# A kernel of attention, eight experts and an MLP: two copies of an expert's products, 192 or 224 columns, chosen at run time by the length of its list

## The chip, the cores and the metric

The kernel is one program on one core of a Trainium2 chip. The metric is the device time of an execution in microseconds, median over several. The engines are PE (TensorE, the matrix engine; PEld is its loading of weights), DVE (VectorE), ACT (ScalarE), POOL (GpSimd) and SP (SyncE, here an issuer of DMAs). Each engine runs its own list of instructions in order and waits on semaphores for the others.

## The reference

Three stages follow one another, all in fp32 at the interface. The first is a decayed linear attention over 2 x 768 positions with 8 heads of 64. Its result, 1536 rows of 512, goes through a mixture of eight experts with one expert per row:

```
logits = xn @ en.T / tau                  # xn, en: rows scaled to length 1
expert_idx = np.argmax(logits, axis=1)
gate_w = probs[np.arange(N), expert_idx]
for e in range(E):
    mask = expert_idx == e
    h = np.maximum(x[mask] @ w1[e], 0.0)              # 512 -> 1024
    out[mask] = gate_w[mask, None] * (h @ w2[e])      # 1024 -> 512
```

The last stage is an MLP over all rows: `h = x @ w_in` (512 -> 2048), `g = elu(h)`, `g @ w_out`. The inputs come from a fixed seed. Worked out from them with the reference's own routing, the lists of the eight experts hold 188, 174, 195, 218, 200, 209, 177 and 175 rows.

## The kernel before, in words

**Products.** Every fp32 product is made of three f16 ones: each operand is split in a high and a low f16 part, and high x high, high x low and low x high are summed in PSUM. An expert's rows are gathered as columns of a tile with room for CAP = 224 of them; rows beyond 224 would be handled by an overflow loop at the end, which is empty for these inputs and is jumped over. Layer 1 of an expert (function `layer1`, line 949) is 96 matmuls of 128x128 weights against 224 columns: four groups `fp` of 24, each into one PSUM tile `ph`. Layer 2 (`layer2`, line 990) is 96 too, in two groups `mp2` of 48, each into one PSUM tile `py`. Each matmul has a weight load of its own. Behind each group ACT writes the high part of the result and DVE the low part, `h` (L957, L972) or `yT` (L996, L1000); the column at which an expert's part of `yT` begins is loaded by ACT and DVE from the table `offi` (L981).

**Order of the experts.** The loop over e emits layer 1 of expert e and then layer 2 of expert e - 1, so PE's order is L1(0), L1(1), L2(0), L1(2), L2(1) and so on to L1(7), L2(6), L2(7). Between groups, `tick` lets the generator `preparing` emit a bounded number of steps that split raw fp32 weights into f16 (ACT L157, DVE L161), and with them new loads of raw weights on SP (L135). The weights of the MLP are loaded and split in the same way.

**Routing.** In expert 0, after its second matmul group of 12, `route_end` makes the index lists (PE L758, DVE L762), and POOL gathers the rows of expert 1 (L769); for expert 1 PE transposes them (L933), for later ones a DMA does (L928). The generator `route_sorted` makes what else is needed of the lists. Its first step sums the routing masks (`ms`); the second adds them up over the partitions on PE (`op`, L784) and makes the counts `cnt` and the starts `off`, `offi` on DVE (L787 to L794). Its later steps sort the index list for the scatter of the output, write the gate values to memory and read them back as `bc` (DMAs of POOL), and make the overflow table (L1115 to L1152). Before the change layer 1 calls `next(self.sorting, None)` at the groups with odd `fp` of every expert from 1 on, and that is the only place where these steps are emitted.

**Tiles of PSUM.** `mm` takes a tile from a ring of four banks; the pool `ps_a` holds four more under the tag "acc", in turn for `py`, for small matmuls and, in the MLP, for the output's accumulators.

## Time and profile before

| | us |
|---|---|
| median of 3 runs (lowest, highest) | 506.09 (504.83, 507.26) |
| the profiled execution, its own time | 507.02 |
| its span in the trace | 505.1 |
| attention stage | 0 to 88.3 |
| expert stage | 88.3 to 245.9 |
| MLP stage, with the empty overflow loop | 245.9 to 505.1 |
| PE busy (share of the span) | 471.9 (93%) |
| DVE busy | 345.1 (68%) |
| ACT busy | 230.1 (46%) |

The profiled execution lies inside the range of the timed ones. Its mean granted clock of PE is 0.971 of full speed. The shares are means over three stages that differ; the rows further below are from single stages.

### The profile page before, as it was taken

The page shows a single profiled execution, that of the slowest core. Times are in us where ns is not written, and L with a number is a line of the kernel's source. Part 1 is how long each engine was busy: PE and PEld are TensorE (multiplying, and loading weights), DVE is VectorE, ACT ScalarE, POOL GpSimd, SP SyncE. Part 2 cuts the span into 40 slices and gives each one's busy share as a digit, 9 for nine tenths or more (in the row PEclk, how much of TensorE's full clock was granted, in tenths as well). Part 3 has the DMA queues.
Part 4 walks back from the last instruction along what each step waited for, and adds up shares of the span by engine and source line. Part 5 has one row for each costly group of instructions (what it writes and reads, how often), then busy time and mean ns, then how long its engine had stood idle before and what let it go on. Part 6 is the DMA issues. An engine that isn't in the chain of part 4 may idle for free. (4 is left out here: it accounts for less than half of the span.)

```text
span 505.1 us, 9103 instructions
## 1 busy us (share of the span) xinstructions
PE 471.9 (93%) x3678; PEld 332.3 (66%) x3678; DVE 345.1 (68%) x612; ACT 230.1 (46%) x382; POOL 73.0 (14%) x66
## 2 busy tenths in 40 slices
PE   6789976689999999999999999999999999999993
PEld 6688865589999999999644444444444444445561
DVE  3469775849999957999787897889544435345352
ACT  1156433768785665333364444535242333333341
POOL 4359520502103100000000000000000003003020
PEclk9799987979999999999999999999999999999997
DMA  6999923599999979956522220000000002002010
GB/s 220 377 404 405 404 96 126 202 283 307 303 381 295 345 289 307 328 182 215 190 84 83 84 84 1 0 1 1 0 1 0 1 0 84 0 2 84 1 62 27
DMA packets 27959, 79.09 MB, mean 157 GB/s; under 512 B 13280, under 2 KB 14848, under 8 KB 21768
## 3 DMA queue, kind: packets, MB, share of 16 engines
q1 hardware_dynamic: 25280, 70.63, 41.2%
q0 software_dynamic: 2288, 7.61, 4.2%
q8 instruction: 31, 0.51, 0.4%
q10 hardware_dynamic: 344, 0.21, 0.2%
q14 instruction: 16, 0.13, 0.1%
HBM read 68.33 MB, written 7.36 MB: 150 GB/s over the span
## 5 line engine op out<-in xcount | busy, mean ns | idle before, releaser
L1034 PE MATMUL pf<-yT,w 128*128 128x512 f16 (+2 forms) x672 | 133.4, 349 | 0.6 <-DVE yT L1000 0.6
L1074 PE MATMUL po<-w,g 128*128 128x512 f16 x576 | 133.3, 379 | 0.3 <-DVE g L1060 0.3
L1034 PEld LDWEIGHTS <-w 128*128 128x128 f16 x672 | 62.4, 98 | 66.0 <-issue 0.9
L1044 DVE TENSOR_TENSOR et<-pf,bc 128x512 f32<-128x512 f32 (+2 forms) x56 | 34.4, 615 | 97.0 <-PE pf L1034 94.8
L1074 PEld LDWEIGHTS <-g 128*128 128x128 f16 x576 | 55.9, 98 | 66.1 <-DVE g L1060 1.2
L1045 ACT ACTIVATE eu<-et 128x512 f32<-128x512 f32 (+2 forms) x56 | 31.9, 569 | 139.8 <-DVE et L1044 139.8
L161 DVE SCALAR_TENSOR_TENSOR w<-raw,w 128x1024 f16<-128x1024 f32 x64 | 76.6, 1228 | 17.8 <-ACT w L157 17.8
L949 PE MATMUL ph<-x,w 128*128 128x224 f16 x768 | 76.9, 262 | 0.5 <-DVE x L749 0.5
L949 PEld LDWEIGHTS <-w 128*128 128x128 f16 x768 | 74.6, 99 | 1.5 <-issue 0.7
L990 PE MATMUL py<-h,w 128*128 128x224 f16 x768 | 74.7, 259 | 0.0
L990 PEld LDWEIGHTS <-w 128*128 128x128 f16 x768 | 73.4, 98 | 0.2 <-issue 0.2
L157 ACT ACTIVATE w<-raw 128x1024 f16<-128x1024 f32 x64 | 64.4, 1051 | 2.2 <-DVE cs L882 2.1
L1093 POOL DMA_INDIRECT out<-o,idx x12 | 12.0, 1004 | 285.4 <-DVE o L1091 276.8
L769 POOL DMA_INDIRECT g<-rows,idx x16 | 22.8, 1428 | 91.0 <-DMA x<-g 60.0
L1060 DVE SCALAR_TENSOR_TENSOR g<-et,g 128x512 f16<-128x512 f32 (+2 forms) x56 | 34.0, 608 | 0.2 <-ACT g L1054 0.2
L1053 DVE SCALAR_TENSOR_TENSOR et<-eu,et 128x512 f32<-128x512 f32 (+2 forms) x56 | 33.9, 605 | 0.3 <-ACT eu L1046 0.3
L1046 ACT ACTIVATE eu<-eu 128x512 f32<-128x512 f32 (+2 forms) x56 | 31.9, 570 | 1.8
L1054 ACT ACTIVATE g<-et 128x512 f16<-128x512 f32 (+2 forms) x56 | 30.9, 552 | 0.2 <-DVE et L1053 0.2
L157 ACT ACTIVATE w<-cv 128x1024 f16<-128x1024 f32 x16 | 16.9, 1054 | 23.7 <-DVE cv L226 23.7
L957 ACT ACTIVATE h<-ph 128x448 f16<-128x448 f32 x32 | 16.7, 541 | 11.2 <-PE ph L949 11.2
L996 ACT ACTIVATE yT<-py 128x448 f32 (+1 forms) x16 | 8.7, 541 | 24.7 <-PE py L990 19.9
L226 DVE SCALAR_TENSOR_TENSOR cv<-raw,cv 128x1024 int32<-128x1024 int32 x16 | 19.5, 1220 | 0.2
(187 smaller groups left out, 405.8 us busy)
## 6 DMA issues: line engine op xcount, KB each, us to landing
raw<-w SPq DMA_DIRECT2D x32, 1024.0 KB, 6.8
in<-qkv SPq DMA_DIRECT2D x16, 512.0 KB, 6.7
raw<-wi SPq DMA_DIRECT2D x8, 1024.0 KB, 5.0
raw<-wo SPq DMA_DIRECT2D x8, 1024.0 KB, 5.1
win<-qkv SPq DMA_DIRECT2D x8, 512.0 KB, 10.6
rows<-row SPq DMA_DIRECT2D x16, 256.0 KB, 7.4
bc<-cd POOLq DMA_DIRECT2D x1, 768.0 KB, 7.7
Dm<-Z SPq DMA_DIRECT2D x1, 512.0 KB, 4.2
```

Source lines behind the costliest of these rows:

```text
L157: nc.scalar.activation(out=o[0], in_=x, func=AF.Copy, scale=sc)
L161: nc.vector.scalar_tensor_tensor(out=o[1], in0=x, scalar=sc, in1=o[0], op0=ALU.mult, op1=ALU.subtract)
L949: nc.tensor.matmul(ps[:, j, :], w[:, wl, k, c : c + P], x[:, xl * KD + k, :], start=(n == 0), stop=(n == 11))
L990: nc.tensor.matmul(ps[:, j, :], w[:, wl, f % 4, c : c + P], h[:, hl, f, :], start=(n == 0), stop=(n == 23))
L1034: nc.tensor.matmul(ps[:, :n], w[:, wl, k, c : c + P], yT[yl][:, k, t0 : t0 + n], start=(i == 0), stop=(i == 11))
L1044: nc.vector.tensor_tensor(out=t[:, :n], in0=UT[m, f][:, :n], in1=self.bc[:, t0 : t0 + n], op=ALU.mult)
L1045: nc.scalar.activation(out=u[:, :n], in_=t[:, :n], func=AF.Relu, scale=-1.0)
L1046: nc.scalar.activation(out=u[:, :n], in_=u[:, :n], func=AF.Exp, scale=-1.0)
L1053: nc.vector.scalar_tensor_tensor(out=t, in0=u, scalar=-1.0, in1=t, op0=ALU.add, op1=ALU.max)
L1054: nc.scalar.activation(out=g[:, 0, :n], in_=t, func=AF.Copy, scale=S_G)
L1060: nc.vector.scalar_tensor_tensor(out=g[:, 1, :n], in0=t, scalar=S_G, in1=g[:, 0, :n], op0=ALU.mult, op1=ALU.subtract)
L1074: nc.tensor.matmul(acc[t], g[:, gl, t * P : t * P + P], w[:, wl, f % 4, :], start=(f == first and i == 0), stop=(f == last and i == 2),)
```

## The change

For experts 1 to 7 PE's products of a layer exist twice in its program, over 192 and over 224 columns. Before each layer PE loads one number (`width[e]`, 1 where the list is longer than 192) and branches to one of the copies. The other engines have no second copy: the groups' waits and releases stand in both copies, so each group of 24 or 48 matmuls still releases its writers by itself. Expert 0 runs 224 columns without a branch. Since both copies write the same tiles, these are allotted once: four tiles `ph` in the ring's four banks, two `py` under a tag of their own, with two left for "acc". The width flags are made in `route_sorted` right behind `offi`; its first two steps are now emitted in expert 0 behind `route_end`, and with the calls in layer 1 left as they were, all later steps come one expert earlier.

```diff
+WIDTHS = (192, CAP)
+    def widths(self, e):
+        if e == 0:
+            yield CAP
+            return
+        i = self.nc.tensor.value_load(self.width[0:1, e : e + 1], min_val=0, max_val=len(WIDTHS) - 1)
+        with self.tc.If(i == 0) as narrow:
+            yield WIDTHS[0]
+        with narrow.Else():
+            yield WIDTHS[-1]
...
+        nc.vector.tensor_scalar(out=self.width, in0=self.cnt, scalar1=float(WIDTHS[0]), scalar2=None, op0=ALU.is_gt)
...
-        ps_a = pool("ps_a", 4, space=PSUM)
+        ps_a = pool("ps_a", 2, space=PSUM)
...
+        ph = [mm([P, 2, CAP], f"ph{i}") for i in range(4)]
+        py = [ps_a.tile([P, 2, CAP], F32, name=f"py{i}", tag="py") for i in range(2)]
...
-                ps = mm([P, 2, CAP], f"ph{e}_{fp}")
-                for j in range(2):
...
+                if fp == 0 or e == 0:
+                    hs = range(4) if e else [fp]
+                    pss = {i: ph[i] for i in hs}
+                    ws = {i: self.need(4 * e + i // 2) for i in hs}
+                    for cols in self.widths(e):
+                        for i in hs:
+                            for j in range(2):
...
+                                        nc.tensor.matmul(
+                                            pss[i][:, j, 0:cols], ws[i][:, wl, k, c : c + P], x[:, xl * KD + k, 0:cols],
...
+                    if e == 0 and fp == 0:
                         self.route_end(ps_a)
+                        next(self.sorting)
+                        next(self.sorting)
                         self.tick(3.0)
...
-            for mp2 in range(2):
-                ps = ps_a.tile([P, 2, CAP], F32, name=f"py{e}_{mp2}", tag="acc")
...
+            pss = py
+            ws = [self.need(4 * e + 2 + i) for i in range(2)]
+            for cols in self.widths(e):
+                for m in range(4):
```

On PE, layer 1 of expert 1 followed directly on the last group of expert 0 (`ph_3`, weights `w_523`):

```order
L949 LDWEIGHTS w_523
L949 MATMUL ph_3_1243<-x_946,w_523 128x224
L949 LDWEIGHTS w_896
L949 MATMUL ph_0_1279<-x_1215,w_896 128x224
L949 LDWEIGHTS w_896
L949 MATMUL ph_0_1279<-x_1215,w_896 128x224
```

At the same place of the changed program (its line 971 is the layer 1, 782 and 783 are the load and the branch):

```order
L971 LDWEIGHTS w_523
L971 MATMUL ph_1093<-x_946,w_523 128x224
L782 TENSOR_LOAD width
L782 ISA x2
L783 COMPARE_AND_BRANCH
L971 LDWEIGHTS w_896
L971 MATMUL ph_1090<-x_1241,w_896 128x192
L971 LDWEIGHTS w_896
```

Four instructions now stand between the two groups, and the first copy has 192 columns. On PE again, after 192 rows of the narrow copy of expert 1's layer 2 (line 1015) comes the jump over the wide copy:

```order
L1015 MATMUL py_1095<-h_1303,w_1563 128x192
L1015 LDWEIGHTS w_1563
L1015 MATMUL py_1095<-h_1303,w_1563 128x192
L783 UNCONDITIONAL_BRANCH
L1015 LDWEIGHTS w_1541
L1015 MATMUL py_1094<-h_1303,w_1541 128x224
```

That jump passes 192 rows of the wide copy and its closing branch, and lands on the head of layer 1 of expert 3, here with the wide copy's end before it:

```order
L1015 LDWEIGHTS w_1563
L1015 MATMUL py_1095<-h_1303,w_1563 128x224
L783 UNCONDITIONAL_BRANCH
L782 TENSOR_LOAD width
L782 ISA x2
L783 COMPARE_AND_BRANCH
L971 LDWEIGHTS w_1668
L971 MATMUL ph_1090<-x_1889,w_1668 128x192
```

PE's list as a whole goes from 6790 to 9548 rows. On DVE, behind the cast of the index list in expert 0, four splits of weights (L161) followed before:

```order
L762 CAST idx<-ip 128x16
L161 SCALAR_TENSOR_TENSOR w_896<-raw_427,w_896 128x1024
L161 SCALAR_TENSOR_TENSOR w_1138<-raw_492,w_1138 128x1024 x2
L161 SCALAR_TENSOR_TENSOR w_1145<-raw_526,w_1145 128x1024
L972 SCALAR_TENSOR_TENSOR h_1093<-ph_0_1094,h_1093 128x448
```

In the changed program the two steps of `route_sorted` and the width flags stand ahead of them:

```order
L764 CAST idx<-ip 128x16
L792 TENSOR_REDUCE ms<-M 128x8
L794 CAST ms_1145<-ms 128x8
L800 COPY cnt<-op 128x8
L801 MEMSET off 128x1
L803 TENSOR_TENSOR off<-off,cnt 128x1 x7
L805 COPY offf<-off 128x8
L807 CAST offi<-off 128x8
L809 TENSOR_SCALAR width<-cnt 128x8
L163 SCALAR_TENSOR_TENSOR w_896<-raw_427,w_896 128x1024
```

Fourteen instructions moved ahead of the splits (now L163), and `cnt` waits there for PE's small matmul `op`, which moved along.

## Rows read from the trace of the kernel before

**Rows 1.** Windows: span, us; busy us of each engine; PEclk; DMA share; GB/s.

```profile
88.30:245.90 157.60, 151.69 (x1579) 150.00 (x1579) 136.64 (x223) 94.10 (x125) 21.88 (x16) 0.98 0.88 284
201.70:248.20 46.50, 45.90 (x471) 44.91 (x469) 45.43 (x72) 16.62 (x24) 0.00 (x0) 1.00 0.72 233
245.90:505.10 259.20, 249.54 (x1250) 117.83 (x1248) 152.13 (x238) 102.88 (x185) 12.04 (x12) 0.99 0.10 33
```

**Rows 2.** Timeline of PE in the expert stage: start, us, then the group.

```profile
134.73 9.36 PE L990 MATMUL py<-h,w 128*128 128x224 f16 x96
143.93 9.36 PE L949 MATMUL ph<-x,w 128*128 128x224 f16 x96
...
227.52 18.56 PE L990 MATMUL py<-h,w 128*128 128x224 f16 x192
```

**Rows 3.** Timeline of PE near the end of the MLP.

```profile
484.44 0.83 PE L1034 MATMUL pf<-yT,w 128*128 128x128 f16 x12
485.11 2.11 PE L1074 MATMUL po<-w,g 128*128 128x512 f16 x9
```

**Rows 4.** Instructions of lines 1161, 981, 1182: ns min/median/max, first and last start.

```profile
L1161 PEldq TENSOR_LOAD <-nu x1: 487/487/487, 495.7 to 495.7; - x1
...
L981 DVEq FUSED_REGOPS  x7: 190/190/206, 138.9 to 239.4; - x7
...
L1182 PEldq COMPARE_BRANCH  x3: 101/197/3347, 496.4 to 501.9; - x3
```

**Rows 5.** The same view, line 949, from 159 to 162.3 us.

```profile
L949 PEldq EVENT_SEMAPHORE  x1: 51/51/51, 160.6 to 160.6; - x1
L949 PEld LDWEIGHTS <-w x1: 97/97/97, 162.2 to 162.2; 128*128 128x128 f16 x1
```

**Rows 6.** The same view, line 1182 (overflow loop), whole span, then 497 to 499.

```profile
L1182 DVEq COMPARE_BRANCH  x3: 41/51/61, 496.8 to 501.8; - x3
...
L1182 PEldq COMPARE_BRANCH  x1: 3347/3347/3347, 496.7 to 496.7; - x1
```

**Rows 7.** DMA queue of instructions: packets, MB, share; whole span, then 496.6 to 500.1.

```profile
q8 instruction: 31, 0.51, 0.4%
...
q8 instruction: 1, 0.02, 1.7%
```

**Rows 8.** Windows between starts of instruction packets (columns as in rows 1).

```profile
205.75:215.56 9.81, 9.81 (x105) 9.81 (x104) 9.05 (x33) 1.09 (x2) 0.00 (x0) 1.00 0.98 271
215.56:229.97 14.41, 14.41 (x153) 14.41 (x151) 14.31 (x18) 5.78 (x9) 0.00 (x0) 1.00 0.65 218
...
259.15:286.79 27.64, 27.64 (x130) 12.54 (x128) 22.24 (x29) 13.82 (x22) 0.00 (x0) 1.00 0.34 114
```

**Rows 9.** PE in the attention stage: timeline with idle time before, and windows.

```profile
65.42 0.18 PE L680 MATMUL kr<-oha,ohb 128*128 128x2 f16 x1 [2.11 <-DVE nrm L451]
...
65.80:69.20 3.40, 3.40 (x29) 3.16 (x26) 2.07 (x4) 0.55 (x1) 2.39 (x3) 0.50 0.24 58
...
81.09 0.17 PE L640 MATMUL kr<-M,c 128*128 128x8 f16 x1 [3.30 <-DVE M L629]
...
79.40:86.30 6.90, 5.21 (x47) 4.57 (x47) 3.35 (x13) 1.58 (x4) 0.00 (x0) 0.51 0.21 78
```

**Rows 10.** Timeline of DVE: list starts, overflow table (first and last), an eviction.

```profile
116.96 1.32 DVE L790 TENSOR_TENSOR off<-off,cnt 128x1 f32<-128x1 f32 x7
...
207.32 0.15 DVE L1115 TENSOR_SCALAR ov<-cnt 1x8 f32<-1x8 f32 x1
...
213.08 0.13 DVE L1152 CAST nu<-ce 1x1 int32<-1x1 f32 x1
...
237.56 0.61 DVE L1000 SCALAR_TENSOR_TENSOR yT<-py,yT 128x448 f32 x1
```

**Rows 11.** Timeline of PE in expert 0, with its waits for gathered rows.

```profile
98.32 0.62 PE L933 MATMUL pt<-c,g 128*128 128x128 f16 x8 [2.44 <-DMA g<-rows,idx]
102.33 0.82 PE L933 MATMUL pt<-c,g 96*128 96x96 f16 x8 [3.39 <-DMA g<-rows,idx]
```

## The prediction

> **What bounds the kernel now.** I read the stages first, in windows: in the expert stage TensorE (PE) is busy 151.69 of 157.60 us and in the MLP stage 249.54 of 259.20, at a granted clock of 0.98 and 0.99 [rows 1]. So in both stages the time is PE's instruction stream. VectorE (DVE) comes next: 136.64 of 157.60 us, and 45.43 of 46.50 in the last three experts [rows 1]. The timeline of PE then shows that stream as an unbroken row of 96-matmul groups, one group per layer and expert, the next starting 9.20 us after the last (134.73 to 143.93): 95.8 ns a matmul of 224 columns [rows 2]. Nothing that only relieves DVE, ACT or the queues can show; shorter matmuls can, and so can anything that makes PE's sequencer late.

> **Columns.** At the end of the program twelve matmuls of 128 columns, each with a weight load of its own, take from 484.44 to 485.11: 0.67/12 = 55.8 ns [rows 3]. Against 95.8 ns that is 40.0 ns for 96 columns, 0.417 ns a column, with no fixed part that would keep 192 columns from paying: 95.8 - 32 x 0.417 = 82.5 ns, 13.3 ns less. By the reference's own routing the eight lists hold 188, 174, 195, 218, 200, 209, 177 and 175 tokens; expert 0 always runs 224, so experts 1, 6 and 7 are narrow and 2 to 5 wide. 3 x 192 matmuls x 13.3 ns = **-7.7 us** (bounds -7 and -8). The most the change can give by its idea is thus 1.5%.

> **Heads.** Each of the 14 blocks (experts 1 to 7, two layers) begins on PE with a load of one number, two register instructions and a compare with branch. Nearest rows: PE's one load of a number took 487 ns, a pair of register instructions on DVE 190, PE's median branch 197 [rows 4]; about 0.9 us, 1.1 with gaps. PE's sequencer runs ahead of its array: a wait that it passed at 160.6 stands before a weight load that began at 162.2, 1.6 us later [rows 5]. While the head runs, the array works that queue off. I cost the heads at **0**, with the cover just wide enough; without it they would be 14 x 1.1 = +15 us.

> **Code.** This is the term that decides. PE's program grows from 6790 to 9548 rows, and a block takes 390 places in it (4 of head, 192 + 1, 192 + 1) of which it walks 197 and jumps 193. What does a jump cost? DVE's branches of the tail, the taken one over its part of the overflow loop among them, took 41 to 61 ns; PE's, over some 890 instructions of that loop, took 3347 ns [rows 6], and one packet of the instruction queue falls into it [rows 7]. The page's queue row has 31 such packets for 0.51 MB [rows 7], 16 KB each. Cut at the starts of these packets, the MLP stage has exactly 128 weight loads a piece, thus 256 instructions, one packet per 256; in the expert stage it has 104 to 151 [rows 8]. I read from this that code comes in pages of 256 instructions, that the next page is asked for when a page is entered, and that a page not there costs F, 3.35 us from the request on, of which PE has up to 1.6 us of lead to set against it. The uneven 104 to 151 say that the request is served up to 24 pairs (2.3 us) late where the other queues are full (DMA share 0.98 in the stretch with 104, 0.34 in the quiet one) [rows 8]; so F lies between 3.35 and 5.65 there. Before, a page lasts 256 x 47.9 ns = 12.3 us and nothing of it shows. After, 390 places go by in 8 to 9 us, a page in 5 to 6, and a page that holds a skip whole is left after 63 places, 3.0 us.

> A narrow block jumps at its end, over the wide copy; a wide one at its start, over the narrow copy. Where a wide block follows a narrow one, the two jumps are five instructions apart and skip 386 places, a page and a half. By the order of the layers this happens twice: second layer of expert 1 to first layer of expert 3 (about 150 us), and first layer of 6 to second layer of 5 (about 217 us). The page landed on was asked for only on reaching those five instructions, so PE stands for F less what is left of its lead. I walked the whole list of PE's instructions with these rules, page by page. At F = 3.35 it waits 2.2 and 1.7 us at the two double jumps and 0.5 elsewhere: 4.4. At F = 4.7, it waits 3.6 and 3.0 there and five times 0.3 to 0.9 after single jumps, where 3.0 us of walking and a lead not yet rebuilt fall short: **+9.5**. At 5.65 some 17. I take 4.7, nearer to the full queues, since the share is still 0.98 up to 215 us and 0.65 after [rows 8].

> [...]

> **Clock.** A stall also has an aftermath. PE stood 2.11 us before 65.42, and the stretch from 65.80 to 69.20 then ran at 0.50, the lower of the two levels; it stood 3.30 us before 81.09, inside a stretch of 6.90 us at 0.51 [rows 9]. Half speed costs half of those stretches, 1.7 to 3.4 us. Two stalls of 3 us or more: 3.4 to 6.8, and 0 if they stay well under 2.11. I take **+4**.

> **The moved routing steps.** The sums of the lists and the width flags go to expert 0, ahead of DVE's weight splits; the seven additions alone took 1.32 us at 116.96 [rows 10], all of it about 2.5. PE's small matmul for them comes up to 1 us late, before two waits of 2.44 and 3.39 us for gathered rows that are there anyway [rows 11], so it is hidden. Splits and with them the raw weight loads move back by the same 2.5 us, which can let those gathers land earlier: 0 to -3, taken as **-1**. The other steps come an expert earlier; the overflow table, DVE 207.32 to 213.08 [rows 10], with them, out of the stretch where DVE has least room.

> **Fixed banks.** The accumulators of the second layer are now two tiles instead of four. Only experts 6 and 7 run second layers back to back: 227.52, 192 matmuls [rows 2], so the last one starts at 236.7, and DVE emptied a tile of expert 6 only from 237.56 [rows 10]. With the overflow table gone from there DVE is earlier, with 7.9 instead of 9.2 us it has less time: 0 to +3, taken as **+0.5**.

> **The sum.** -7.7 + 0 + 9.5 + 4 - 1 + 0.5 = +5.3 on the profiled execution's 507.0, which stands 0.9 above the median of 506.1: 511.4, say **511.5 us**. With F from 3.35 without clock (506.1 - 8.2 + 4.4 = 502.3) to 5.65 with 6.8 of clock (521.7), this case alone reaches from 502 to 522.

> **The rivals.** *Code never late.* If more than the next page lies ready, the decisive point being 386 places of skip, no jump waits: 506.1 - 7.7 - 1 + 0.5 = 498, faster. For it: no wait for code can be seen in 12.3 us per page, and the packets' landing is not the request. Against it: PE's jump of 890 cost 3347 ns with a packet inside, so the store ahead ends before 890, and behind that jump no second packet came at once. [...] Chance 0.33. *The effects cancel*, 503.6 to 508.6: F near 3.35 with one of the two stalls followed by a low clock (502.3 + 1.7 to 3.4), or code in time but DVE, busy 45.43 of 46.50 us [rows 1], holds the narrow experts 6 and 7 to the old pace, which loses 5.1 of the 7.7 us: 503. Chance 0.17. *The flags do nothing*: were all lists over 192, the columns would give 0, the skips would all be single, and the time 506 to 509; the routing counts speak against it, under 0.02. *Heads uncovered* would add up to 15 us, to 525; the lead of 1.6 us speaks against it, 0.05, inside the forecast's side.

> **How the numbers follow.** About 0.5% (2.5 us) is what a measurement here can tell from no change: faster is below 503.6, slower above 508.6. The forecast has 0.5, nearly all of it slower; code in time 0.33, all faster; cancelled 0.17, some of it below 503.6. Faster 0.35, same 0.15, slower 0.50. The range must hold both sides: from 497.5, a little under the rival's 498, to 520, which leaves out only the upper end of the code term with the whole price of the clock.

> **What would show it.** Right: matmuls of experts 1, 6 and 7 at 82 to 83 ns, others at 95.8; two PE gaps of 2 to 4 us at about 150 and 217 us right behind a jump, with an instruction packet landing just before they end and a clock of 0.5 behind; packets 5 to 6 us apart. Wrong if the MLP stage begins 6 to 9 us before 245.9 with no gap at the jumps, or if PE stands at every head by about a microsecond, or if waits for DVE in experts 6 and 7 take the gain.

## The result and the profile after

| | before | after |
|---|---|---|
| median (lowest, highest), us | 505.46 (504.48, 507.26) | 511.32 (508.83, 512.58) |
| profiled execution, its span, us | 507.02, 505.1 | 511.16, 509.4 |
| expert stage on PE, us | 88.27 to 245.92 | 86.57 to 251.46 |

The ratio is 1.0106 (95% interval 1.0056 to 1.0155): slower by about 1%. All ratios here go by the runs within 1.5% of the fastest of their kernel; one kernel below had three longer ones. The window of the expert stage, span first, then busy time by engine, PE's granted clock, DMA share and GB/s, answer to [rows 1]:

```profile
86.57:251.46 164.89, 148.19 (x1580) 143.71 (x1580) 138.81 (x225) 94.92 (x125) 19.31 (x16) 0.97 0.85 273
```

The stage is 7 us longer, though PE is busy 3.5 us less in it. So matmuls did get shorter, and PE now stands idle. Where it stands is read in the timeline of PE of the changed kernel (start, us, line, count, and in brackets the idle time before and what ended it by the semaphores); it answers to [rows 2, 11]:

```profile
91.15 0.17 PE L797 MATMUL op<-ms,c 128*128 128x8 f16 x1 [1.59 <-DVE ms L794]
91.17 6.42 PE L971 MATMUL ph<-x,w 128*128 128x224 f16 x48
97.43 0.95 PE L952 MATMUL pt<-c,g 128*128 128x128 f16 x16
...
120.12 9.36 PE L971 MATMUL ph<-x,w 128*128 128x224 f16 x96 [2.12 <-ACT yT L1024]
129.32 8.08 PE L1015 MATMUL py<-h,w 128*128 128x192 f16 x96
141.99 11.02 PE L971 MATMUL ph<-x,w 128*128 128x224 f16 x96 [4.59 <-DVE w L163]
152.85 0.51 PE L877 MATMUL sp<-rhs,wohb 128*128 128x60 bf16 x12
153.37 3.82 PE L1015 MATMUL py<-h,w 128*128 128x224 f16 x38
157.45 5.72 PE L1015 MATMUL py<-h,w 128*128 128x224 f16 x58 [0.27 <-issue]
163.87 9.36 PE L971 MATMUL ph<-x,w 128*128 128x224 f16 x96 [0.70 <-ACT yT L1024]
...
173.50 3.05 PE L1015 MATMUL py<-h,w 128*128 128x224 f16 x30
180.66 7.95 PE L1015 MATMUL py<-h,w 128*128 128x224 f16 x66 [4.10 <-issue]
...
197.64 2.46 PE L1015 MATMUL py<-h,w 128*128 128x224 f16 x24
200.91 7.07 PE L1015 MATMUL py<-h,w 128*128 128x224 f16 x72 [0.81 <-issue]
207.82 8.08 PE L971 MATMUL ph<-x,w 128*128 128x192 f16 x96
215.74 1.89 PE L1015 MATMUL py<-h,w 128*128 128x224 f16 x18
219.14 7.65 PE L1015 MATMUL py<-h,w 128*128 128x224 f16 x78 [1.50 <-issue]
...
235.61 16.01 PE L1015 MATMUL py<-h,w 128*128 128x192 f16 x192 [0.91 <-ACT h L983]
```

Three things are to be seen. The transposes of expert 1 no longer wait for gathered rows: the 2.44 and 3.39 us of [rows 11] are gone, and a wait of 1.59 us for the moved sums has come ahead of them. A narrow layer takes 7.92 us (207.82 to 215.74) instead of 9.20: 82.5 ns a matmul. And behind expert 0 stand eight gaps, 15.0 us together, where [rows 2] had none. Some fall between two layers, at a seam, and carry the name of DVE or ACT, some in the middle of a copy with nothing to wait for ("issue").

The four in mid-copy are worth a count. PE's list of instructions has two places for a matmul and its weight load. From the gap after 30 matmuls of layer 2 of expert 3 to that after 24 of expert 4 it is 66 x 2 + 1 to the end of the copy, 390 for the block between, 4 of head, 193 of the copy jumped over, and 24 x 2: 768 = 3 x 256. From 38 of expert 2 to 30 of expert 3, and from 24 of expert 4 to 18 of expert 5, it is 768 again (116 + 1 + 390 + 4 for a small product + 4 + 193 + 60, and 144 + 1 + 390 + 4 + 193 + 36). With a packet per 256 instructions [rows 8] that is three pages each time, so I read these gaps as standing at page ends.

For the gaps at the seams, the durations of single branches at line 783 (min/median/max in ns, start in us):

```profile
L783 PEldq COMPARE_BRANCH  x1: 3116/3116/3116, 116.8 to 116.8; - x1
L783 PEldq COMPARE_BRANCH  x1: 4930/4930/4930, 136.9 to 136.9; - x1
...
L783 PEldq COMPARE_BRANCH  x1: 1703/1703/1703, 162.0 to 162.0; - x1
L783 PEldq COMPARE_BRANCH  x1: 317/317/317, 172.9 to 172.9; - x1
...
L783 PEldq COMPARE_BRANCH  x1: 1639/1639/1639, 233.1 to 233.1; - x1
```

Of the 20 branches of this line the six that fall through took 0.07 to 0.09 us and ten jumps 0.22 to 0.41; those at the gaps of 2.12, 4.59, 0.70 and 0.91 took 1.6 to 4.9. The granted clock behind the two longest gaps, in windows from the gap to the end of the group (columns as above):

```profile
142.00:152.90 10.90, 10.90 (x98) 10.25 (x99) 7.25 (x9) 5.13 (x7) 0.86 (x1) 0.84 1.07 334
180.66:188.44 7.78, 7.78 (x66) 7.21 (x67) 1.76 (x2) 1.49 (x2) 2.58 (x3) 0.81 0.77 282
```

Layer 1 of expert 3 takes 10.86 us from 141.99 to 152.85 instead of 9.20, and 66 matmuls 7.78 instead of 6.32: 3.1 us for the clock (0.61 from 142.00 to 145.40 and 0.56 from 180.70 to 184.10, most of it at the lower of the two levels in the trace, 0.50 and 1.00). Behind the other gaps the pitch is as ever: 9.20 us for the group after 2.12, 6.91 for 72 matmuls after 0.81.

### The profile page after: what moved, and what is told of

Read it like the earlier page. It is cut to its first block, busy times and chain, and to the rows that moved or that the text cites. A ratio compares the mean times of both kernels' runs of the same rounds, so it can differ in the third digit from the quotient of the medians.

```text
span 509.4 us, 9182 instructions
## 1 busy us (share of the span) xinstructions
PE 469.5 (92%) x3678; PEld 327.2 (64%) x3678; DVE 346.3 (68%) x613; ACT 230.9 (45%) x382; POOL 70.4 (14%) x66
## 5 line engine op out<-in xcount | busy, mean ns | idle before, releaser
L1062 PEld LDWEIGHTS <-w 128*128 128x128 f16 x672 | 62.4, 98 | 65.4 <-issue 0.2
L163 DVE SCALAR_TENSOR_TENSOR w<-raw,w 128x1024 f16<-128x1024 f32 x64 | 76.9, 1228 | 18.5 <-ACT w L159 18.4
L971 PE MATMUL ph<-x,w 128*128 128x224 f16 (+1 forms) x768 | 74.7, 261 | 8.0 <-DVE w L163 4.6
L1015 PE MATMUL py<-h,w 128*128 128x224 f16 (+1 forms) x768 | 73.1, 257 | 7.6 <-issue 6.7
L971 PEld LDWEIGHTS <-w 128*128 128x128 f16 x768 | 71.6, 100 | 11.6 <-issue 7.0
L1015 PEld LDWEIGHTS <-w 128*128 128x128 f16 x768 | 70.1, 99 | 9.7 <-issue 7.8
L771 POOL DMA_INDIRECT g<-rows,idx x16 | 20.2, 1266 | 72.7 <-DMA x<-g 42.7
L998 DVE SCALAR_TENSOR_TENSOR h<-ph,h 128x448 f16<-128x448 f32 x32 | 19.6, 616 | 2.0 <-ACT h L983 1.9
```

The lines of the kernel that those rows point to most:

```text
L163: nc.vector.scalar_tensor_tensor(out=o[1], in0=x, scalar=sc, in1=o[0], op0=ALU.mult, op1=ALU.subtract)
L971: nc.tensor.matmul(pss[i][:, j, 0:cols], ws[i][:, wl, k, c : c + P], x[:, xl * KD + k, 0:cols], start=(n == 0), stop=(n == 11),)
L1015: nc.tensor.matmul(pss[m // 2][:, m % 2, 0:cols], ws[f // 4][:, wl, f % 4, m * P : m * P + P], h[:, hl, f, 0:cols], start=(n == 0), stop=( ...
L1062: nc.tensor.matmul(ps[:, :n], w[:, wl, k, c : c + P], yT[yl][:, k, t0 : t0 + n], start=(i == 0), stop=(i == 11))
```

## The experiments

Theory A: PE waits for its own code, after jumps and in mid-copy. Rivals: B, the seams' gaps are data waits, as their releasers say; C, the moved steps and fixed banks are neutral, and the gather waits vanished by chance; D, the heads cost. For the vanished gather waits: E, the raw weight loads start later; F, the fixed banks; G, the steps' earlier place.

### Columns without a branch

```diff
     def widths(self, e):
...
+        yield WIDTHS[0] if e in (1, 6, 7) else CAP
```

> One copy of each layer's products and no branch; 192 columns for experts 1, 6 and 7 and 224 for the others are fixed when the program is built, which holds for these inputs' lists alone. Fixed banks and moved routing steps stay. Theory A (code pages that come late after jumps, and the low clock behind the two long ones, cost the 15 us of waits and some 3 us of clock seen in the changed kernel's trace): all gaps at the seams vanish, 511.3 - 15 - 1.3 (ends of the pipeline at the gaps) - 3 = 492 us, 491 to 494. Rival B (the gaps before layer 1 of experts 2, 3 and 4, which the trace puts down to DVE and ACT, are waits for split weights and evictions that come late in the new order): they stay, 8 us with their clock, and the time is 499 to 501.

Measured: 493.57 us, ratio to before 0.9746 (0.9715 to 0.9776). PE's timeline of this kernel has the same narrow layers and no idle time behind the transposes but 0.49 us:

```profile
102.59 8.08 PE L963 MATMUL ph<-x,w 128*128 128x192 f16 x96 [0.49 <-ACT x L945]
110.51 9.36 PE L1007 MATMUL py<-h,w 128*128 128x224 f16 x96
119.71 9.36 PE L963 MATMUL ph<-x,w 128*128 128x224 f16 x96
128.91 8.08 PE L1007 MATMUL py<-h,w 128*128 128x192 f16 x96
136.83 9.36 PE L963 MATMUL ph<-x,w 128*128 128x224 f16 x96
```

All eight gaps are gone, though nothing was taken out but PE's loads of a width, its branches and the second copies; DVE's width flags stand as before. B falls: a releaser is the semaphore that came last before the engine went on, and at 141.99 it had come during a wait for something else: the branch of 136.9 lasted up to 141.8.

### One copy of 224 columns

```diff
     def widths(self, e):
...
+        yield CAP
```

> One copy over 224 columns for every expert, no branch, no load of a width; fixed banks and moved routing steps stay. All theories that put the columns at 7.7 us: static columns plus 7.7. Theory A: 500 us (499 to 502), so 5 to 6 us under the kernel before, all of it from the two waits for gathered rows in expert 0 (2.44 and 3.39 us with their low clock) that are gone in the changed kernel. Rival C (those waits vanished by chance, the moved steps and fixed banks are neutral): 505 to 506.5.

Measured: 500.38 us, 0.9882 (0.9851 to 0.9913). Without any narrow column the moved steps and fixed banks alone gain 5.8 us; C falls. Against the fixed columns it is 6.8 us slower by the medians, the pitch says 7.7; the runs of each spread over 1.6 to 1.7 us.

### Two copies of 224 columns: alternating, and always the first

```diff
         with self.tc.If(i == 0) as narrow:
-            yield WIDTHS[0]
+            yield CAP
```

> The changed kernel with 224 columns in both copies; the compare, the branches and all jumps are the same, narrow experts take the first copy and wide ones the second. Theory A: the same page walk, a little slower pages in the three experts: 13 us of waits and 2 to 4 us of clock over the single copy, 514 to 518. Rival D (the heads, a load and a compare of about 0.7 us each on PE's sequencer, are what costs, not where the jump lands): the single copy plus 14 x 0.7 to 1.1, 510 to 516, equal to the kernel in which every block takes its first copy.

For the second kernel also:

```diff
-        nc.vector.tensor_scalar(out=self.width, in0=self.cnt, scalar1=float(WIDTHS[0]), scalar2=None, op0=ALU.is_gt)
+        nc.vector.tensor_scalar(out=self.width, in0=self.cnt, scalar1=float(N), scalar2=None, op0=ALU.is_gt)
```

> As the alternating kernel (two copies of 224 columns, same heads), but the width flag is set only above 1536, so all 14 blocks take their first copy and jump at their end: no two jumps ever follow each other without 197 instructions between them. Theory A: the two double jumps and their clock are gone, single jumps remain, 7 to 9 us of waits over the single copy: 506 to 510, and 6 to 9 us under the alternating kernel. Rival D: equal to the alternating kernel within 1.5 us.

Measured: alternating 522.93 us, 1.0339 (1.0302 to 1.0377); always the first copy 0.9993 (0.9965 to 1.0022), with seven runs from 502.63 to 507.46 us (median 506.02) and three more from 511.08 to 513.27 (all ten: 506.74). Same copies, same heads, the same work on PE, and 16 to 17 us between them: only where the branch goes differs. D alone can't give that. In the alternating kernel the long gaps stand at the seam of the first double jump and one page end behind the second:

```profile
145.08 11.96 PE L971 MATMUL ph<-x,w 128*128 128x224 f16 x96 [4.70 <-DVE w L163]
...
217.79 1.89 PE L1015 MATMUL py<-h,w 128*128 128x224 f16 x18
223.85 10.12 PE L1015 MATMUL py<-h,w 128*128 128x224 f16 x78 [4.17 <-issue]
```

Both are followed by a low clock (0.77 from 145.08 to 156.88 and 0.74 from 223.85 to 233.81; 11.96 us against the usual 9.36, and 10.12 for 78 matmuls against 7.65 in the changed kernel). The alternating kernel is 22.5 us over the single copy where I expected 15 to 17, the other 5.6 (6.4 by all ten runs) where I expected 7 to 9. Single jumps are not free; the kernel that has only these stands in mid-copy too, after 25 matmuls and 768 places later after 7 (142 + 1 + 193 + 390 + 24 + 4 + 14):

```profile
129.23 2.56 PE L1015 MATMUL py<-h,w 128*128 128x224 f16 x25
134.15 6.98 PE L1015 MATMUL py<-h,w 128*128 128x224 f16 x71 [2.36 <-issue]
...
150.97 0.83 PE L1015 MATMUL py<-h,w 128*128 128x224 f16 x7
153.58 8.70 PE L1015 MATMUL py<-h,w 128*128 128x224 f16 x89 [1.78 <-issue]
```

### Heads with short copies

```diff
-                    for cols in self.widths(e):
-                        for i in hs:
+                    for cols, i in ((c, q) for q in hs for c in (self.widths(e) if q == 0 else [CAP])):
```

(both copies of 224 columns; layer 2 likewise, by its four m)

> The same 14 heads (load, two register instructions, compare) as in the changed kernel, with the same alternation, but only the first 24 of a block's 96 matmuls stand in two copies, both of 224 columns; the other 72 stand once. Code grows by a quarter of what it grows in the change. Theory A: pages last 9 us or more, no waits: the 500.4 us of the single copy, 499.5 to 502. Rival D: 14 heads of 0.7 to 1.1 us exposed: 510 to 516.

Measured: 500.43 us, 0.9888 (0.9856 to 0.9921), against 500.38 without any head. Fourteen heads cost nothing that can be seen, as a lead like that of [rows 5] would have it. D falls for the change as it stands.

### Smaller copies

Each block is cut in two, three or four, with its own branch. Half blocks:

```diff
-                    for cols in self.widths(e):
-                        for i in hs:
+                    for cols, i0 in ((c, q) for q in hs[::2] for c in self.widths(e)):
+                        for i in hs[i0 - hs[0] : i0 - hs[0] + 2]:
```

> The changed kernel (192 or 224 columns by the width flag) with each block cut in two: 28 heads instead of 14, and a jump passes 97 places instead of 193, a double jump 198 instead of 386. Theory A (late code pages): no page is left after a handful of instructions any more, so only short waits of under 1 us each remain, 3 to 7 us together with no low clock behind them, over the 493.6 us of the fixed columns: 497 to 501. Rival D (heads cost): twice the heads, so more waits than in the changed kernel, 512 to 528.

Quarter blocks with one load a layer (the load moved into a function `width_of`, called once a layer):

```diff
+                    for cols, i in ((c, q) for r in [self.width_of(e)] for q in hs for c in self.widths(r)):
```

> As half blocks, but cut in four (24 matmuls a copy, jumps of 49 places), and the width is loaded once per layer; only the compare and branch stand before each quarter. Theory A: the walk through the pages is nearly even, 256 places in 5.3 to 6.2 us: 0 to 3 us of waits over the fixed columns, and 56 branches of 0.07 to 0.3 us on a sequencer that runs 1.6 us ahead: 494 to 498. Rival D: 4 branches a layer cost more than one, over 505.

Half blocks, with one load a layer in the same way:

> Half blocks with the width loaded once a layer instead of once a block; the copies and jumps are the same. Theory A: the waits hang on the pages, so as half blocks, 497 to 500. Rival D: 14 loads and register instructions of 0.5 us less, 7 us under half blocks, 491 to 493.

Three quarters of the products in two copies:

```diff
+                    for cols, part in ((c, q) for q in ((0, 1), (2,), (3,)) for c in ([CAP] if q == (3,) else self.widths(e))):
+                        for i in [i for i in hs if i in part]:
```

> The changed kernel with three quarters of a layer's matmuls in two copies (a block of 48 and one of 24) and the last 24 once over 224 columns: 342 places a layer instead of 390, jumps of 97 and 49. Theory A: 1.9 of the 7.7 us of columns are given up, the pages last 6 to 6.5 us, waits of 1 to 4 us: 493.6 + 1.9 + 1 to 4 = 496.5 to 499.5. Rival D (heads, 28 of them): 510 or more.

| | us | ratio to before (95%) |
|---|---|---|
| half blocks | 498.73 | 0.9867 (0.9821 to 0.9914) |
| half blocks, one load | 499.85 | 0.9883 (0.9845 to 0.9921) |
| quarter blocks, one load | 500.18 | 0.9878 (0.9846 to 0.9910) |
| three quarters | 496.84 | 0.9815 (0.9767 to 0.9863) |

All four keep the choice at run time and beat both kernels. Half blocks instead of whole ones give back 12.6 us with twice the heads; one load instead of two gains nothing. Quarters missed their 494 to 498: an even walk through the pages still waits (1.76 and 2.06 us in its profile with no data wait named), 6.6 us over the fixed columns, presumably since the same 390 places go by in the same 8 to 9 us. Less code seems to help more: three quarters waits least in the profiles (0.65 and 1.28 us at two seams) and has the lowest median of the versions that choose at run time, though it gives up a quarter of the columns; its interval overlaps that of half blocks. Half blocks with one load still had, in its profile, a single branch of 5.3 us, with an instruction packet between 150 and 151 us and 3.47 us of PE's time lost behind it:

```profile
L788 PEldq COMPARE_BRANCH  x1: 5277/5277/5277, 148.0 to 148.0; - x1
```

### Where the gather waits went

Single copy, the two routing steps behind the splits:

```diff
                         self.route_end(ps_a)
-                        next(self.sorting)
-                        next(self.sorting)
                         self.tick(3.0)
+                        next(self.sorting)
+                        next(self.sorting)
```

> The single copy of 224 columns with the two routing steps of expert 0 emitted behind the weight splits of that place instead of ahead of them. Theory E (the two waits for gathered rows vanished because the splits, and behind them the raw weight loads, start 2 us later and leave the DMA engines to the gathers): splits and loads start early again, the waits of 2 to 6 us with their low clock come back, 504 to 507. Rival F (the fixed banks or the earlier routing steps took them away): 500 to 501.5 as before.

Measured: 503.37 us, 0.9965 (0.9944 to 0.9985). A little under the range of E, and it doesn't decide: PE now waits for the sums, which DVE makes behind four splits, and that wait stands in place of the gathers'.

```profile
95.26 0.17 PE L789 MATMUL op<-ms,c 128*128 128x8 f16 x1 [4.17 <-DVE ms L786]
```

So I left the steps where they were before, and put in a pause alone (one copy of 224 columns in both kernels).

```diff
                         self.route_end(ps_a)
+                        pad = rp.tile([P, 2], F32, name="pad")
+                        nc.vector.memset(pad, 0.0)
+                        for _ in range(14):
+                            nc.vector.tensor_tensor(out=pad[:, 1:2], in0=pad[:, 0:1], in1=pad[:, 1:2], op=ALU.add)
-                        next(self.sorting)
-                        next(self.sorting)
                         self.tick(3.0)
```

Without the pause (these two have no width flags either):

> The kernel before with the tiles of the change: fixed banks, one copy of 224 columns, no width flags, and the routing steps at their old place (from expert 1 on). If the moved steps are what took the waits for gathered rows away (theories E and G): the kernel before, 505 to 507, with the two waits of 2 to 3.5 us ahead of the transposes. If the fixed banks did (rival F): 500 to 501.5.

With it:

> As banks only, with 14 additions of one column on DVE (about 2.6 us, their result is not used) between the cast of the index list and the weight splits of expert 0; no routing step is moved. Theory E (the splits, and behind them the raw weight loads, start later, so the gathers have the DMA engines to themselves): the waits vanish as with the moved steps, 500 to 502. Theory G (it is the steps themselves, coming earlier, and with them the writes of later experts): 505 to 507, as banks only, or later by up to 2.6 us.

Measured: 506.69 us, 1.0015 (0.9997 to 1.0032), without; 500.40 us, 0.9887 (0.9841 to 0.9934), with. Some 2.6 us of additions on DVE, whose result nobody reads, make the kernel 6.3 us faster. The timelines of PE, POOL and SP show why (for SP, the time is that to the last start), and below each the DMA queues in the 2.8 us behind the first gather's issue (91.70 to 94.50, and with the pause 92.50 to 95.30; packets, MB, share; q0 moves the gathers, q1 the raw weights). Without the pause:

```profile
96.19 0.62 PE L942 MATMUL pt<-c,g 128*128 128x128 f16 x8 [2.20 <-DMA g<-rows,idx]
100.06 0.82 PE L942 MATMUL pt<-c,g 96*128 96x96 f16 x8 [3.25 <-DMA g<-rows,idx]
...
89.92 1.74 POOL L771 DMA_INDIRECT g<-rows,idx  x1 [20.55 <-DVE idx L764]
91.97 1.87 POOL L771 DMA_INDIRECT g<-rows,idx  x1 [0.31 <-issue]
...
90.81 13.48 SPq L137 DMA_DIRECT2D raw<-w  x4
...
q1 hardware_dynamic: 111, 0.91, 100.2%
...
236.30 3.90 PE L1003 MATMUL py<-h,w 128*128 128x224 f16 x39 [1.34 <-DVE yT L1016]
```

With the pause:

```profile
95.35 1.17 PE L942 MATMUL pt<-c,g 128*128 128x128 f16 x16
...
91.45 1.01 POOL L771 DMA_INDIRECT g<-rows,idx  x1 [21.64 <-DVE idx L764]
92.77 0.92 POOL L771 DMA_INDIRECT g<-rows,idx  x1 [0.30 <-issue]
...
95.75 8.73 SPq L137 DMA_DIRECT2D raw<-w  x4
...
q0 software_dynamic: 137, 0.45, 51.3%
```

Without it a load of 1 MB of raw weights starts 0.9 us after the first gather is issued and 1.2 us before the second; with it, the first load comes 4.3 us behind the first gather. In the first stretch not one packet of the gathers moved and 0.91 MB of raw weights did; in the second it was the gathers alone. E is shown, F and G fall. One thing isn't separated: the pause also moves DVE's four splits, from 89.57 to 94.50 us, and POOL issued the first two gathers in 1.01 and 0.92 us instead of 1.74 and 1.87, so part of the waits can be the splits' own doing. The row at 236.30 shows the price of two fixed banks: layer 2 of expert 7 waits 1.34 us for DVE. Where the overflow table has moved forward, as in the changed kernel and the single copy, that wait isn't there.

## Why the prediction was right

The mechanism was: the columns come, the heads are covered, and PE then waits for pages of code that are not there in time. All three are shown, the third by the eight gaps (15.0 us, a packet of code ahead of each) and by their absence from the kernel with one copy. That the sum of 511.5 meets 511.32 so closely is luck: two of its terms were mis-sized in opposite directions.

| term | predicted | measured, from what |
|---|---|---|
| columns | -7.7 | -7.7 (7.92 us a layer for 9.20, six layers); -6.8 by medians |
| heads | 0 | 0.05, short copies against the single copy |
| waits for code | +9.5 | +15.0, the eight gaps |
| clock | +4 | +3.1, two stretches |
| moved steps | -1 | -5.8 to -6.3, single copy against before and against banks only |
| fixed banks | +0.5 | +0.7 alone (the interval of its ratio holds 1), 0 in the change |

The measured terms add up to +4.6 of the +5.9 between the medians. Each gap also lets the pipeline run empty, 0.16 us (a group of 96 takes 9.36, the next one follows after 9.20): 1.3 us for eight, which closes the sum.

**Waits for code.** The place was right for the first double jump (4.59 us at 141.99, predicted 3.6 at about 150) and half right for the second: the jump itself took 0.23 us, and the wait came at the next page end (1.50 us at 219.14). Two gaps the walk didn't have so: 2.12 us at 120.12, and 4.10 at 180.66, where it gave under 0.9. How much of that is due to the walk's page ends, which only the mid-copy gaps give exactly, is not known. But one F for all pages doesn't hold. Packets of the instruction queue start within 139.4 to 139.5, 178.2 to 178.3, 198.3 to 198.4 and 216.9 to 217.0 (the DMA view of these four windows: packets, MB, share):

```profile
q8 instruction: 1, 0.02, 56.5%
...
q8 instruction: 1, 0.02, 61.5%
...
q8 instruction: 1, 0.02, 69.7%
...
q8 instruction: 1, 0.02, 58.3%
```

PE runs again at 141.99, 180.66, 200.91 and 219.14, each time 2.2 to 2.6 us behind the packet's start. The other four gaps have a packet too, within 117.4 to 117.5, 155.0 to 155.1, 161.3 to 161.4 and 232.4 to 232.5, 2.4 to 3.2 us ahead of PE's next matmul. If the page is asked for on entering the one before, the count of places puts that at the heads of 136.2, 171.6 and 214.7 and some 11 places (half a microsecond) ahead of that of 195.9. The packet then starts 3.2, 6.6, 2.2 and about 2.9 us after it, and F is 5.8, 9.1, 4.4 and about 5.5 us. The 4.7 that I took lies among three of them; the late one cost its 4.10 us and the low clock after it. That the request is made at that moment, which the walk took for granted, was an assumption of mine: the traces show when a packet starts (one per 256 instructions in the MLP stage [rows 8]), not what asks for it. Why one packet started 6.6 us after is open. The sign "packets 5 to 6 us apart" did not come: 18 packets from 129.5 to 251.0 are one in 6.8 us, since PE stands in between.

**Single jumps.** The walk gave them 0.3 to 0.9 us a time, in five places. In the kernel with single jumps only PE stood 2.36 and 1.78 us in mid-copy, so they are not free: the page with the jump ahead of the first gap holds 63 places that are run, 3.0 us at 47.9 ns, and the next one isn't there. How much code lies ready ahead of PE was measured by no run; the 4.59 us behind a skip of 386 places say only that the code landed on there was not ready.

**Clock.** Two gaps over 4 us were answered by a low clock, as in [rows 9], and cost 1.66 and 1.46 us; the gap of 2.12 wasn't. The length of a gap alone doesn't say it: behind the 1.59 us for the sums, 48 matmuls took 6.42 us instead of 4.76 (granted clock 0.73 from 91.17 to 97.40), while in the kernel with fixed columns the same gap of 1.59 was followed by 48 in 4.76.

**Moved steps.** I bounded this from 0 to -3 and the truth lay outside. I had the mechanism (later splits, later raw loads, gathers that land earlier) but took it as a shift by 2.5 us. What it removes is a collision. The 5.8 us is not simply the two waits, though they add up to 5.83. In the profiles of before and of the single copy,

```profile
91.12 4.76 PE L949 MATMUL ph<-x,w 128*128 128x224 f16 x48
...
102.95 13.51 PE L949 MATMUL ph<-x,w 128*128 128x224 f16 x120
...
98.68 11.86 PE L963 MATMUL ph<-x,w 128*128 128x224 f16 x120
```

the half-speed stretch behind the waits goes as well (13.51 to 11.86; its granted clock was 0.50 from 102.95 to 106.35), but the wait for the sums and the low clock behind it, which I had called hidden, cost 3.2 us. From the start of the expert stage to the second layer of expert 0 this nets 4.7 us (28.06 to 23.35); 0.8 more comes at the head of the MLP stage, whose first 48 matmuls took 11.14 us before, with a wait of 0.62 for DVE, and 10.37 in the single copy.

**The rivals.** Code never late would have been the 493.6 us of the fixed columns, with the moved steps at their true size; it was refuted by the gaps. The cancelling case didn't come. That the releasers were named DVE and ACT at the seams spoke for data waits and was misleading.

## What to carry to other kernels

A second copy of unrolled code can cost the engine that walks it even if the jump is cheap (here ten of 0.22 to 0.41 us): whole copies of 224 columns stood 5.6 us over the single copy with single jumps and 22.5 with double ones, copies of a quarter of a block 0.05. Count the instructions between page ends (256 places) that are really executed, and keep their time well above what a page takes to arrive under load, here 4.4 to 5.8 us and once 9.1 if it is counted as above (5.8 us are 121 matmuls and loads of 47.9 ns); quarters, whose pages last 5.3 to 6.2 us by estimate, still waited. Cut the copies small and leave part of the work uncopied (498.73 and 496.84 us here for 511.32). A transfer that the critical engine waits for should not share its first microseconds with bulk loads that nobody needs yet: a pause, or cheap work moved there, can be worth more than the change it was moved for (500.40 against 506.69 us here). When a gap's releaser is a data semaphore, compare with the same program without the suspected cause before believing it.
